# Attention output product of eleven instead of twelve passes through spare rows, and the filter's last feature products turned round, with their constants as weights

## The chip, the core and the metric

The kernel runs on one core of a Trainium2 chip. The metric is device time in microseconds (us) of one execution. Engines in the profile: PE (TensorE matmul) and PEld (its weight loads), DVE (VectorE), ACT (ScalarE), POOL (GpSimd) and SP (SyncE); POOL and SP here mainly issue DMAs.

## The reference

Two independent results are written side by side. The left half is attention of 16 heads with one shared key and value head; the right half is a spectral filter (a 2-D FFT, a product with a complex filter, the inverse FFT).

```python
B, S, D, H = 1, 2048, 448, 16           # head size Dh = 28
q = (x @ wq).reshape(B, S, H, Dh).transpose(0, 2, 1, 3)
k, v = x @ wk, x @ wv
p = softmax(einsum("bhqd,bkd->bhqk", q, k) * Dh ** -0.5)
a = einsum("bhqk,bkd->bhqd", p, v).transpose(0, 2, 1, 3).reshape(B, S, H * Dh) @ wo
...
X = rfft2(x2, axes=(-2, -1)) * (w_r + 1j * w_i)
b = irfft2(X, s=(S, D), axes=(-2, -1))
out = concatenate([a, b], axis=-1)
```

## The kernel before

**Layout.** The 16 heads are four groups g of four heads, each head padded from 28 to 32 rows, so that a group fills 128 partitions. The 2048 queries are four chunks c of 512. For each (c, g) the 2048 keys are 16 blocks kc of 128: 256 *steps* in all. A step has four score products (one a head, 128 keys by 512 queries, float32r, in `score`, L1100), four exponentials of 128 by 512 on ACT (`exps`, L1117, into a buffer `p`), and four value products (`values`, L1132, fp32, 32 rows each, into PSUM bank 7). Banks 0 to 6 are shared by scores and by filling work. There are `P_BUFS` = 20 buffers `p`; an exponential can't begin before its buffer and its scores are there, and a buffer is free again when the value products of its step have read it.

**Precision by parts.** Where a float32r product alone is too coarse, an operand is split into a high part and a remainder (`oh`, `ol` for the attention result, `woh`, `wol` for the output weights), and three products are added: high by high, remainder by high, high by remainder.

**Filling work.** Two kinds of work are put on PE between the scores. A *W unit* (`w_unit`, `wo_mm`, L1020) is the output product of 128 queries: four groups g, three float32r products of 448 columns each, twelve in all; DVE copies the bank out (L1024) and SP stores it. *Z and Y units* are the filter's last stage, for eight blocks q. Z (`z_unit`, L942): four fp32 products, weights are the filter data, moving are the constants `fi`; DVE copies the result to SBUF (L948). Y (`y_unit`, L961): the results of Z are the weights, the constants `cs3` (113 by 113) are moving, four fp32 products of 113 columns; DVE makes sums and differences (L966 to L968, L974, L975), and SP stores 128 rows of 4 by 113. Their buffers are carved out of `X`, the 28.9 KB a partition in which the filter's middle part ran on DVE until then.

**Order.** All engines run in a fixed order that the kernel's own planner writes while it is built: `clk` holds planned clocks, `after` a heap of planned events for DVE and DMA, `background` the filter's DVE work. The main loop at the end of the kernel issues scores while a bank is free, and value products in a batch of 2 steps, or of 4 when filling work is there (`size`). I call what lies between the starts of two batches a *round*: a short round has 8 scores and ends with the value products of 2 steps, a long one has 15 to 17 scores, filling work in two or three places, and ends with the value products of 4 steps. How much is filled in a long round is set by `share`: at least 1.6 us of planned time, more when the steps run out. At the end the third chunk's leftovers and 36 products of the last chunk (`partial`) follow the last value products.

**Around a group's end.** `group_out` (L986) copies bank 7 out, the sums of the exponentials go through DRAM (POOL's DMAs `sd`, `rs`, `rd`, `R`), and `group_norm` (L1008, L1010, L1011) multiplies and splits. When the fourth group of a chunk is done, the chunk's four W units can start.

Of the kernel before, what the change touches and what calls it, by code (L numbers as in the profile page):

```python
# [12 lines left out]
F32 = mybir.dt.float32  # L13
# [4 lines left out]
ALU = mybir.AluOpType  # L18
# [13 lines left out]
P_BUFS = 20  # L32
# [63 lines left out]
def kernel(ctx: ExitStack, tc: tile.TileContext, t: dict):  # L96
# [14 lines left out]
    X = cp.tile([128, 2, 32, 113], F32, name="X")  # L111
# [101 lines left out]
    with tc.tile_pool(name="f1", bufs=2) as f1[0], tc.tile_pool(name="w1", bufs=1) as w1, ExitStack() as ctx1:  # L213
# [146 lines left out]
        def load_const(name, shape):  # L360
            def go():
                cons[name] = cp.tile(shape, F32, name=name)
                nc.sync.dma_start(cons[name], t[name])
            return add(SP, 0.4, go, loads[1, 1], kb=32)
# [297 lines left out]
    pp = ctx.enter_context(tc.tile_pool(name="pp", bufs=P_BUFS))  # L662
    V = nc.vector
# [8 lines left out]
    def after(when, dur, f, *a):  # L672
        heapq.heappush(events, (when, next(serial), dur, f, a))
# [17 lines left out]
    woh = ap.tile([128, NG, D], F32R, name="woh", bufs=1)  # L691
    wol = ap.tile([128, NG, D], F32R, name="wol", bufs=1)
    fc["cs3"] = ap.tile([113, 4, 113], F32, name="cs3", bufs=1)
    nc.gpsimd.dma_start(fc["cs3"], t["cs3"])
# [66 lines left out]
    def wo_split(g):  # L761
        V.tensor_copy(woh[:, g], wo[g])
        TT(wol[:, g], wo[g], woh[:, g].bitcast(F32), op=ALU.subtract)
# [145 lines left out]
    Xf = X.rearrange("p r n f -> p (r n f)")  # L909
    taken = [0]  # L910

    def carve(p, n):
        o = taken[0]
        taken[0] += n
        return Xf[:p, o:o + n]

    c2t = [carve(128, 904).rearrange("p (u j f) -> p u j f", u=2, f=113) for _ in range(2)]
    fit = [carve(128, 512).rearrange("p (j f) -> p j f", f=128) for _ in range(2)]
    zt = [[carve(113, 512).rearrange("p (r j n) -> p r j n", r=2, n=64) for _ in range(2)] for _ in range(2)]
    mt = [carve(128, 226).rearrange("p (k f) -> p k f", f=113) for _ in range(2)]  # L920
    y1t = [carve(128, 452).rearrange("p (k h f) -> p k h f", k=2, f=113) for _ in range(2)]
    yot = [carve(128, 452).rearrange("p (k f) -> p k f", f=113) for _ in range(2)]
# [6 lines left out]
    def fft3_load(q):  # L929
        if q > 7:  # L930
            return
        nc.gpsimd.dma_start(c2t[q % 2].rearrange("p u j f -> p u (j f)"), t2[:, :, 452 * q:452 * q + 452])
        nc.gpsimd.dma_start(fit[q % 2], t["fi"][:, 4 * q:4 * q + 4])
        after(clk["dve"] + (10.0 if q < 2 else 6.0), 0.0, work["z"].extend, [z_unit(q, 0), z_unit(q, 1)])

    def z_unit(q, e):
        w = (113, 112)[e]

        def go(b):
            pz = view(bank[b], 4, 128)  # L940
            for j in range(4):
                mm(pz[:w, j], c2t[q % 2][:, e, j, :w], fit[q % 2][:, j], start=True, stop=True)  # L942
            if e == 1:
                after(clk["pe"] + 1.2, 0.0, fft3_load, q + 2)
            after(clk["pe"] + 1.2, 0.72, out, b)
# [6 lines left out]
        return [(0.88, go)]  # L952

    def y_unit(q, v):
        js = slice(2 * v, 2 * v + 2)

        def go(b):
            py = view(bank[b], 4, 113)
            ze, zo = zt[q % 2]
            for k, (z, w, r) in enumerate(((ze, 113, 0), (zo, 112, 0), (zo, 112, 1), (ze, 113, 1))):  # L960
                mm(py[:, k], z[:w, r, js], fc["cs3"][:w, k], start=True, stop=True)  # L961
            after(clk["pe"] + 1.2, 1.2, out, b)

        def out(b):
            py, m, y1 = view(bank[b], 4, 113), mt[v], y1t[v]
            V.tensor_copy(m, py[:, 2:4])  # L966
            TT(y1[:, :, 0], py[:, 0:2], m, op=ALU.add)
            TT(y1[:, :, 1], py[:, 0:2], m, op=ALU.subtract)  # L968
            free[b] = clk["dve"] + 0.1
            after(clk["dve"], 0.8, last)  # L970

        def last():
            y1, yo = y1t[v], yot[v]
            TT(yo[:, 0:2], y1[:, 0], y1[:, 1], op=ALU.add)  # L974
            TT(yo[:, 2:4], y1[:, 0], y1[:, 1], op=ALU.subtract)  # L975
            r0 = (2 * q + v) * 128
            nc.sync.dma_start(t["ob"][r0:r0 + 128], yo)
        return [(0.88, go)]


    oh, ol, osb = {}, {}, {}
# [13 lines left out]
    def group_sums(c, g, rs, rd):  # L995
        V.reciprocal(rs, rs)
        nc.gpsimd.dma_start(rd.rearrange("i (a b) -> (i a) b", b=16), rs)
        R = ap.tile([128, CW], F32, name="R", bufs=1)
        for i in range(4):
            nc.gpsimd.dma_start(R[32 * i:32 * i + 32], rd[i:i + 1].to_broadcast([32, CW]))  # L1000
        after(clk["dve"] + 12.0, 2.1, group_norm, c, g, R)

    def group_norm(c, g, R):
# [4 lines left out]
        TT(o, o, R, op=ALU.mult)  # L1008
        h = oh[c][:, g]
        V.tensor_copy(h, o)  # L1010
        TT(ol[c][:, g], o, h.bitcast(F32), op=ALU.subtract)  # L1011
        normed[c] += 1
        if normed[c] == NG and c < NC - 1:
            after(clk["dve"] + 0.3, 0.0, work["w"].extend, [w_unit(c, k) for k in range(4)])

    def wo_mm(p, c, k, gs):
        s = slice(k * 128, k * 128 + 128)
        for g in gs:
            for n, (x, w) in enumerate(((oh, woh), (ol, woh), (oh, wol))):
                mm(p, x[c][:, g, s], w[:, g], start=(g == 0 and n == 0), stop=(g == NG - 1 and n == 2))  # L1020
# [20 lines left out]
    def w_unit(c, k):  # L1041
# [10 lines left out]
        return [(0.605, go(g)) for g in range(NG)]  # L1052
# [102 lines left out]
    for g in range(NG):  # L1155
        after(w0 + 6 * g, 0.0, wo_load, g)
        after(w0 + 6.0 + 6 * g, 1.1, wo_split, g)
# [81 lines left out]
    nc.sync.dma_start(w3, t["wo"][:, g])  # L1239
# [25 lines left out]
def _constants():  # L1265
# [27 lines left out]
    c["cs3"] = np.stack([we * np.cos(te.T), pad(2.0 / D * np.cos(to.T)), pad(-2.0 / D * np.sin(to.T)),  # L1293
                         -we * np.sin(te.T)], 1)
# [14 lines left out]
def _layout(A_x, A_wq, A_wk, A_wv, A_wo, B_x, B_w_r, B_w_i):  # L1309
# [13 lines left out]
    z["wo"] = wo.reshape(NG, 128, D).transpose(1, 0, 2)  # L1323
# [18 lines left out]
def _gather(oa, ob):  # L1342
    out = np.empty((1, S, 2 * D), np.float32)
    out[0, :, :D] = oa
    y = ob.reshape(32, 64, 4, 113).transpose(1, 0, 2, 3).reshape(S, 4, 113)
# [9 lines left out]
_OUTS = {"oa": (S, D), "ob": (S, 4, 113)}  # L1355
# [16 lines left out]
```

## Time and profile before

| | us |
|---|---|
| runs (three) | 641.3, 644.09, 645.07 |
| median | 644.09 |
| profiled execution, device time | 641.98 |
| its span | 640.1 |
| first value products start | 76.31 |
| last value products start | 624.04 |

The granted clock of PE was 0.999 over the span. In rows of the timeline the columns are start, duration, engine, line, operation, output and inputs, shapes, count, and in brackets how long the engine stood idle before it and what ended that. A PE matmul's duration includes its way through the array; what a stream of them costs is read from start to start.

### The profile page before, as it was taken

How to read it: one execution, taken by the hardware profiler on the slowest of the kernel's cores; microseconds unless marked ns; L12 is line 12 of the kernel's file. 1: busy time of each engine (PE TensorE's matmuls, PEld its weight loads, DVE VectorE, ACT ScalarE, POOL GpSimd, SP SyncE). 2: the span in 40 equal slices, each digit the busy share in tenths (PEclk: the TensorE clock that was granted, in tenths of full speed). 3: DMA queues.
4: the chain of work that ended last, by engine and by line, in shares of the span. 5: the costliest groups of instructions: out<-in, count | busy, mean ns of one | idle time of the engine just before them, and what ended most of it. 6: DMA issues, size and time to landing. Idle time of an engine off the chain costs nothing.

```text
span 640.1 us, 11636 instructions
## 1 busy us (share of the span) xinstructions
PE 633.5 (99%) x4380; PEld 358.5 (56%) x4380; DVE 333.3 (52%) x687; ACT 547.0 (85%) x1100; POOL 89.1 (14%) x164
## 2 busy tenths in 40 slices
PE   9999999999999999999999999999999999999997
PEld 7877544444444456554446655655665655564445
DVE  5999615979897977896323222215334310320014
ACT  4644899999999998889999879878888987888991
POOL 1021131101121101010122020020301101020200
PEclk9999999999999999999999999999999999999999
DMA  8766587030334121124444231132415131130002
GB/s 299 255 164 166 134 239 244 18 68 17 97 105 102 42 68 47 32 67 150 151 141 139 64 91 36 49 111 88 115 61 143 32 82 32 50 93 1 19 0 87
DMA packets 29667, 62.41 MB, mean 98 GB/s; under 512 B 6798, under 2 KB 18415, under 8 KB 28645
## 3 DMA queue, kind: packets, MB, share of 16 engines
q1 hardware_dynamic: 21850, 40.36, 23.1%
q0 software_dynamic: 7328, 20.72, 10.8%
q8 instruction: 35, 0.57, 0.4%
q10 hardware_dynamic: 432, 0.57, 0.3%
q14 instruction: 22, 0.18, 0.1%
HBM read 29.63 MB, written 15.02 MB: 70 GB/s over the span
## 4 chain that ended last, share of the span: by engine, by line
PE 88%; ACT 0%; issue 0%; DVE 0%; ACTq 0%
PE b L1100 41%; PE b L1132 36%; PE b L1020 6%; PE b L961 2%; PE b L942 2%; PE b L1252 0%; PE b L163 0%; ACT yb L1035 0%; DVE yb L1038 0%; ACTq L1036 0%
## 5 line engine op out<-in xcount | busy, mean ns | idle before, releaser
L1117 ACT ACTIVATE p<-b 128x512 f32<-128x512 f32 x1024 | 506.7, 768 | 46.4 <-PE b L1100 45.4
L1100 PE MATMUL b<-qa,ka 128*128 128x512 f32 x1024 | 284.7, 411 | 0.5 <-PEq L617 0.5
L1100 PEld LDWEIGHTS b<-qa,ka 128*128 128x128 f32 x1024 | 182.1, 188 | 128.2 <-ACT p L1117 83.9
L1132 PE MATMUL b<-p,vs 128*32 128x512 f32 x2048 | 240.0, 597 | 0.0
L1132 PEld LDWEIGHTS b<-p,vs 128*32 128x32 f32 x2048 | 56.5, 109 | 120.9 <-issue 119.3
L986 DVE COPY qraw<-b 128x512 f32<-128x512 f32 x15 | 10.4, 692 | 82.0 <-PE b L1132 82.0
L1024 DVE COPY ya<-b 128x448 f32<-128x448 f32 x12 | 7.5, 624 | 65.1 <-PE b L1020 64.0
L991 POOL DMA_DIRECT2D sd<-qraw x15 | 8.8, 587 | 218.8 <-DVE qraw L986 218.8
L827 DVE SCALAR_TENSOR_TENSOR X<-w,X 128x226 f32<-128x226 f32 (+2 forms) x72 | 34.1, 473 | 2.4
L1000 POOL DMA_DIRECT2D R<-rd x60 | 30.2, 508 | 34.9 <-DMA rd<-rs 34.9
L966 DVE COPY X<-b 128x226 f32<-128x226 f32 x16 | 6.2, 390 | 45.3 <-ACT p L1117 43.9
L321 ACT ACTIVATE qraw<-b 128x512 f32<-128x512 f32 x16 | 9.4, 599 | 19.5 <-PE b L317 19.4
L948 DVE COPY X<-b 113x512 f32<-113x512 f32 (+1 forms) x16 | 11.1, 691 | 28.6 <-ACT p L1117 22.7
L317 PE MATMUL b<-xh,wqh 128*128 128x512 f32 x64 | 24.6, 416 | 0.4 <-DVE xh L265 0.4
L1008 DVE TENSOR_TENSOR qraw<-qraw,R 128x512 f32<-128x512 f32 x15 | 10.3, 685 | 26.7 <-DMA R<-rd 26.7
L317 PE MATMUL b<-xh,wql 128*128 128x512 f32 x64 | 23.0, 390 | 0.0
L1020 PE MATMUL b<-woh,oh 128*128 128x448 f32 x60 | 22.1, 369 | 0.0
L1020 PE MATMUL b<-wol,oh 128*128 128x448 f32 x60 | 22.0, 366 | 0.0
L1020 PE MATMUL b<-woh,ol 128*128 128x448 f32 x60 | 21.9, 366 | 0.0
L820 DVE SCALAR_TENSOR_TENSOR w<-X 128x113 f32<-128x113 f32 (+2 forms) x56 | 17.7, 353 | 0.1
L961 PEld LDWEIGHTS b<-cs,X 113*128 113x128 f32 (+1 forms) x128 | 16.8, 191 | 1.4
L317 PE MATMUL b<-xl,wqh 128*128 128x512 f32 x48 | 17.3, 391 | 0.0
(113 smaller groups left out, 511.4 us busy)
## 6 DMA issues: line engine op xcount, KB each, us to landing
qa<-qa SPq DMA_DIRECT2D x15, 512.0 KB
X<-t POOLq DMA_DIRECT2D x16, 452.0 KB, 5.4
xb<-xb SPq DMA_DIRECT2D x8, 512.0 KB
qa<-qh SPq DMA_DIRECT2D x60, 64.0 KB
qa<-ql SPq DMA_DIRECT2D x60, 64.0 KB
R<-rd POOLq DMA_DIRECT2D x60, 64.0 KB, 2.2
t<-bs SPq DMA_DIRECT2D x16, 226.0 KB
wf<-w POOLq DMA_DIRECT2D x8, 452.0 KB, 4.2
```

The source lines that it names most:

```text
L317: mm(pq[c, g], w[:, j, gs], x[:, j], start=(j == 0 and n == 0), stop=(j == 3 and n == 1))
L820: STT(out, y, sy, x, op0=ALU.mult, op1=ALU.add if c > 0 else ALU.subtract)
L827: todo(226 * n, lambda d=d, q=q: STT(both(d), t[0].rearrange("p r n f -> p r (n f)"), q, both(a), op0=ALU.mult, op1=ALU.add))
L942: mm(pz[:w, j], c2t[q % 2][:, e, j, :w], fit[q % 2][:, j], start=True, stop=True)
L948: V.tensor_copy(zt[q % 2][e][:w], view(bank[b], 4, 128)[:w].rearrange("p j (r n) -> p r j n", r=2))
L961: mm(py[:, k], z[:w, r, js], fc["cs3"][:w, k], start=True, stop=True)
L986: V.tensor_copy(o, bank[7])
L1000: nc.gpsimd.dma_start(R[32 * i:32 * i + 32], rd[i:i + 1].to_broadcast([32, CW]))
L1020: mm(p, x[c][:, g, s], w[:, g], start=(g == 0 and n == 0), stop=(g == NG - 1 and n == 2))
L1100: mm(bank[b], ka[:, kc * 128:(kc + 1) * 128], qa[c, g][:, h], start=True, stop=True)
L1117: nc.scalar.activation(p, bank[b], AF.Exp, scale=SCALE)
L1132: mm(bank[7][32 * i:32 * i + 32], vs[:, kc], pt.pop(4 * st + i), start=(kc == 0), stop=(kc == 15))
```

## The change

**Output product.** In chunks 0 to 2 the third product of group 0 (remainder `ol` of group 0 by `woh` of group 0) is dropped. Its 112 real rows are carried by the 4 unused rows in each block of 32 of seven other operands: the remainder of group 0 goes to DRAM (`lows`) and comes back by eight DMAs on SP into rows 28 to 31 of `oh` (all four groups) and of `ol` (groups 1 to 3), and the weights hold the matching rows of group 0, which needs seven weight blocks in `woh` in place of four. A W unit has eleven products. It may start 7 planned us after the last group of its chunk is normalised. Chunk 3 keeps twelve.

**Filter.** In Y the constants, now split into `csh` and `csl` and padded to 128 columns, are the weights; the results of Z, split by DVE into a high part and a remainder, are moving. A Y unit is six float32r products of 256 columns. Both Y units of a block are needed for the last sums, which now are 128 by 512; two stores of 128 rows of 2 KB follow per block. The constants come by a POOL DMA when the filter's middle part has ended, and are split on DVE.

**Memory and planner.** `X` has its space only until the last stage begins, `P_BUFS` is 17, some constants move to an early pool, and the planner's numbers for W, Y and Z are new, with at least 1.8 us in a long round in place of 1.6.

```diff
-P_BUFS = 20
+P_BUFS = 17
...
-    woh = ap.tile([128, NG, D], F32R, name="woh", bufs=1)
+    woh = ap.tile([128, 7, D], F32R, name="woh", bufs=1)
...
+    def fft3_open():
+        xp.close()
+        p3 = xp.enter_context(tc.tile_pool(name="p3", bufs=2))
...
+        cs = scratch()[:, :512].rearrange("p (k f) -> p k f", k=4)
+        nc.gpsimd.dma_start(cs, t["cs3"])
+        todo(512, lambda: V.tensor_copy(csh, cs))
+        todo(512, lambda: TT(csl, cs, csh.bitcast(F32), op=ALU.subtract))
...
-            V.tensor_copy(zt[q % 2][e][:w], view(bank[b], 4, 128)[:w].rearrange("p j (r n) -> p r j n", r=2))
+            pz = view(bank[b], 4, 128)[:w].rearrange("p j (r n) -> p r j n", r=2)
+            h, l = (x[:w] for x in fb["z", q % 2, e])
+            V.tensor_copy(h, pz)
+            TT(l, pz, h.bitcast(F32), op=ALU.subtract)
...
-            for k, (z, w, r) in enumerate(((ze, 113, 0), (zo, 112, 0), (zo, 112, 1), (ze, 113, 1))):
-                mm(py[:, k], z[:w, r, js], fc["cs3"][:w, k], start=True, stop=True)
+            for k in range(2):
+                kind, e, r = ((0, 0, 0), (2, 1, 1), (1, 1, 0), (3, 0, 1))[2 * v + k]
...
+                for n, (c, z) in enumerate(((csh, zh), (csh, zl), (csl, zh))):
+                    mm(py[:, k], c[:w, kind], z, start=(n == 0), stop=(n == 2))
...
+            if g == 0:
+                lows[c] = dp.tile([128, CW], F32, name="lows", bufs=2)
+                nc.sync.dma_start(lows[c], ol[c][:, 0].bitcast(F32))
+            rows = lows[c].rearrange("(i m r) n -> r i m n", i=4, r=4)
+            if g == NG - 1:
+                for r in range(4):
+                    nc.sync.dma_start(oh[c][DH + r::32].bitcast(F32), rows[r, :, :4])
+                    nc.sync.dma_start(ol[c][DH + r::32, 1:].bitcast(F32), rows[r, :, 4:7])
+                after(clk["dve"] + 7.0, 0.0, work["w"].extend, [w_unit(c, k) for k in range(4)])
...
-            for n, (x, w) in enumerate(((oh, woh), (ol, woh), (oh, wol))):
-                mm(p, x[c][:, g, s], w[:, g], start=(g == 0 and n == 0), stop=(g == NG - 1 and n == 2))
+            spare = c < NC - 1
+            for n, (x, w, m) in enumerate(((oh, woh, g), (oh, wol, g), (ol, woh, g + 3 * spare))):
+                if n < 2 or g or not spare:
+                    mm(p, x[c][:, g, s], w[:, m], start=(g == 0 and n == 0), stop=(g == NG - 1 and n == 2))
...
-    total = 12 * 4 * 0.605 + 32 * 0.88
+    total = 12 * 2.22 + 16 * (0.88 + 0.73)
...
-        return max(1.6, n * (total - done[0]) / max(250 - done_steps, 3)) if n > 2 else 0.0
+        return max(1.8, n * (total - done[0]) / max(250 - done_steps, 3)) if n > 2 else 0.0
```

**What it does to the order.** ACT's order is the same throughout; PE's is the same up to step 80. From there the planner packs differently. PE's order, first long round before (`qa`, `ka` are the operands of a score, `b` the banks; the row ahead of the first three output products is the sixth score after the value products):

```order
L1100 MATMUL b_77<-qa_1163,ka 128x512
L1020 MATMUL b_80<-woh,oh 128x448
L1020 MATMUL b_80<-woh,ol 128x448
L1020 MATMUL b_80<-wol,oh 128x448
L1100 MATMUL b_78<-qa_1163,ka 128x512
L1100 MATMUL b_79<-qa_1163,ka 128x512
L1020 MATMUL b_80<-woh,oh 128x448
```

The same place now, from the sixth score of the first long round:

```order
L1124 MATMUL b_77<-qa_1167,ka 128x512
L1044 MATMUL b_78<-woh,oh 128x448
L1044 MATMUL b_78<-wol,oh 128x448
L1124 MATMUL b_80<-qa_1167,ka 128x512
L1124 MATMUL b_81<-qa_1167,ka 128x512
L1044 MATMUL b_78<-woh,oh 128x448
L1044 MATMUL b_78<-wol,oh 128x448
L1044 MATMUL b_78<-woh,ol 128x448
L1124 MATMUL b_82<-qa_1167,ka 128x512
```

The first group's third product is gone, and a round now holds a whole W unit in four places (2, 3, 3 and 3 products) where it held three places of three.

PE's order at the first Y units, before (`X` is where the results of Z lie):

```order
L1100 MATMUL b_78<-qa_128,ka 128x512
L961 MATMUL b_80<-cs_1092,X 128x113 x4
L1100 MATMUL b_82<-qa_128,ka 128x512
L1100 MATMUL b_83<-qa_128,ka 128x512
L961 MATMUL b_81<-cs_1092,X 128x113 x4
```

and now (`zh`, `zl` are the parts of the results of Z):

```order
L1124 MATMUL b_82<-qa_127,ka 128x512
L972 MATMUL b_77<-zh_3809,csh 128x256
L972 MATMUL b_77<-zl_3810,csh 128x256
L972 MATMUL b_77<-zh_3809,csl 128x256
L972 MATMUL b_77<-zh_3811,csh 128x256
L972 MATMUL b_77<-zl_3812,csh 128x256
L972 MATMUL b_77<-zh_3811,csl 128x256
L1124 MATMUL b_78<-qa_127,ka 128x512
L1124 MATMUL b_76<-qa_127,ka 128x512
L972 MATMUL b_81<-zh_3811,csh 128x256
```

Four products became six of another shape; behind the second unit, which begins in the last row, a Z unit follows as a third place in the same round.

DVE's order where the filter's middle part ends, now (`qraw<-qraw,R` begins `group_norm`, `qt<-qraw` begins the split of the next group's queries, `qraw<-b_83` is `group_out`):

```order
L829 SCALAR_TENSOR_TENSOR X<-w,X 128x2x113 x2
L923 CAST csh<-w 128x512
L924 TENSOR_TENSOR csl<-w,csh 128x512
L1022 TENSOR_TENSOR qraw<-qraw,R 128x512
L1024 CAST oh<-qraw 128x512
L1025 TENSOR_TENSOR ol<-qraw,oh 128x512
L195 TENSOR_SCALAR qt<-qraw,mask,cvec 128x512
L196 CAST qh<-qt 128x512
L197 TENSOR_TENSOR ql<-qt,qh 128x512
L1001 COPY qraw<-b_83 128x512
```

The two rows of `csh` and `csl` stand ahead of a group's norm and of the next `group_out`; before, they were not there.

Counted over the whole order of PE, with S scores, W output products, and Y and Z units in a long round:

| | before | now |
|---|---|---|
| short rounds | 68 | 82 |
| long rounds | 30 | 23 |
| stretches of long rounds, by first steps | 80, 128, 208 | 84, 128, 134, 144, 212 |
| output products in long rounds | 141 (47 places) | 129 (12 places of 2, 35 of 3) |
| output products after the last score | 6 + 33 | 3 + 36 |

The long rounds now: 6 of S16 W11 (three of them open a stretch), 2 of S17 W11, 2 of S16 YYZ (one opens a stretch), S15 YYZ, S17 YYZ, S16 ZZZ (opens a stretch), S17 ZZZ, 2 of S15 Z W5, 2 of S16 W6 Y, 2 of S16 Y W8, S16 W3 ZZ, S16 YYY, S15 Y ZZ. Before: 6 of S15 W9, 6 of S15 YY, 2 of S16 W9, 6 of S16 with W6 and a Y or Z, 3 of S17 W9, 5 of S17 ZZ, 2 of S17 W3 ZZ.

More of the change, by code (lines that the diff above doesn't have):

```diff
@@ L952, in z_unit @@
         return [(0.88, go)]
+    y1 = {}
     def y_unit(q, v):
-        js = slice(2 * v, 2 * v + 2)
         def go(b):
-            py = view(bank[b], 4, 113)
-            ze, zo = zt[q % 2]
-            for k, (z, w, r) in enumerate(((ze, 113, 0), (zo, 112, 0), (zo, 112, 1), (ze, 113, 1))):
-                mm(py[:, k], z[:w, r, js], fc["cs3"][:w, k], start=True, stop=True)
-            after(clk["pe"] + 1.2, 1.2, out, b)
-        def out(b):
[L965 to L970, printed above, removed]
@@ new lines, in go @@
+            after(clk["pe"] + 1.2, 2.65 if v else 1.25, out, b)
+        def out(b):
+            py = view(bank[b], 2, 256)
+            y = y1[v] = scratch()[:, :768].rearrange("p (s n) -> p s n", s=3)
+            V.tensor_copy(y[:, 2], py[:, 1])
+            TT(y[:, 0], py[:, 0], y[:, 2], op=ALU.add)
+            TT(y[:, 1], py[:, 0], y[:, 2], op=ALU.subtract)
+            free[b] = clk["dve"] + (-1.3 if v else 0.1)
+            if v:
+                a, c = y1.pop(0), y1.pop(1)
+                for h, op in enumerate((ALU.add, ALU.subtract)):
+                    last(h, op, a, c)
@@ L982, with last @@
+        def last(h, op, a, c):
+            yo = fp.tile([128, 2, 256], F32, name="yo", tag="bs")
+            TT(yo, a[:, :2], c[:, :2], op=op)
+            nc.sync.dma_start(t["ob"][q, h], yo)
+        return [(0.73, go)]
+    oh, ol, osb, lows = {}, {}, {}, {}
+    R = ap.tile([128, CW], F32, name="R", bufs=1)
+    after(12.0, 0.4, V.memset, R, 0.0)
     normed, taken_out = [0] * NC, [0]
@@ L1012, in group_norm @@
         normed[c] += 1
-        if normed[c] == NG and c < NC - 1:
-            after(clk["dve"] + 0.3, 0.0, work["w"].extend, [w_unit(c, k) for k in range(4)])
+        if c < NC - 1:
+            if g == 0:
[7 more added lines that the diff above has]
+                after(clk["dve"] + 7.0, 0.0, work["w"].extend, [w_unit(c, k) for k in range(4)])
     def wo_mm(p, c, k, gs):
@@ L1051, in out @@
             free[b] = clk["dve"] + 0.1
-        return [(0.605, go(g)) for g in range(NG)]
+        return [(0.605 if g else 0.403, go(g)) for g in range(NG)]
     def switch(mode):
@@ L1154 @@
     w0 = 5.0 if FIRST == 8 else 28.0
-    for g in range(NG):
-        after(w0 + 6 * g, 0.0, wo_load, g)
-        after(w0 + 6.0 + 6 * g, 1.1, wo_split, g)
+    for g in range(7):
+        at = w0 + 6 * g if g < NG else 60.0 + 6 * g
+        after(at, 0.0, wo_load, g)
+        after(at + 6.0, 1.1, wo_split, g)
     for q in range(FIRST, 8):
```

73 lines of the change are left out of this document (34 added, 39 removed).

## The prediction

> **What bounds the kernel now.** The page first: PE's share, and the chain that ended last.
>
> ```profile
> span 640.1 us, 11636 instructions
> PE 633.5 (99%) x4380; PEld 358.5 (56%) x4380; DVE 333.3 (52%) x687; ACT 547.0 (85%) x1100; POOL 89.1 (14%) x164
> PE 88%; ACT 0%; issue 0%; DVE 0%; ACTq 0%
> ```
>
> Read alone, this says that PE is the bound and that each us of PE work taken away is a us won. The timeline says otherwise for a part of the run. A short round on PE, and in the second fence ACT over that part:
>
> ```profile
> 123.46 1.92 PE L1132 MATMUL b<-p,vs 128*32 128x512 f32 x16
> 125.31 2.11 PE L1100 MATMUL b<-qa,ka 128*128 128x512 f32 x8
> 127.36 1.92 PE L1132 MATMUL b<-p,vs 128*32 128x512 f32 x16
> ```
>
> ```profile
> 75.69 163.84 ACT L1117 ACTIVATE p<-b 128x512 f32<-128x512 f32 x334
> ```
>
> From 75.69 on ACT runs 334 exponentials without a gap, 0.49 us each; a short round is eight of them, 127.36 - 123.46 = 3.90 (3.96 later on; I take 3.93). There **ACT** is the bound. A long round of 15 scores:
>
> ```profile
> 359.46 3.64 PE L1132 MATMUL b<-p,vs 128*32 128x512 f32 x32
> 363.03 1.67 PE L1100 MATMUL b<-qa,ka 128*128 128x512 f32 x6
> 363.57 5.99 ACT L1117 ACTIVATE p<-b 128x512 f32<-128x512 f32 x12 [1.16 <-PE b L1100]
> 364.54 0.37 PE L1020 MATMUL b<-woh,oh 128*128 128x448 f32 x1
> 364.75 0.36 PE L1020 MATMUL b<-woh,ol 128*128 128x448 f32 x1
> 365.62 0.36 PE L1020 MATMUL b<-woh,oh 128*128 128x448 f32 x1
> 368.14 0.19 PEld L1100 LDWEIGHTS b<-qa,ka 128*128 128x128 f32 x1 [0.20 <-ACT p L1117]
> 368.57 0.64 PE L1132 MATMUL b<-p,vs 128*32 128x512 f32 x4
> ```
>
> It lasts 9.11. Value products hold PE for 3.57 (359.46 to 363.03), ACT runs dry and starts again 4.11 after the round's start. But the last score also waits 0.20 for a bank, which an exponential frees. So a long round has two bounds: PE's own sum, and a **tick of ACT**: 4.11, plus one exponential (5.99 for twelve, 0.50) for each score beyond the banks that scores can use (six while a filling unit holds one), plus the rest to 9.11, 0.50, from the bank to the value products. With 15, 16, 17 scores that is 9.11, 9.61, 10.11. Two more rounds, of 16 and (second fence) of 17 scores:
>
> ```profile
> 246.66 3.64 PE L1132 MATMUL b<-p,vs 128*32 128x512 f32 x32
> 255.34 0.19 PEld L1100 LDWEIGHTS b<-qa,ka 128*128 128x128 f32 x1 [0.19 <-ACT p L1117]
> 255.83 0.19 PEld L1100 LDWEIGHTS b<-qa,ka 128*128 128x128 f32 x1 [0.30 <-ACT p L1117]
> 256.27 1.06 PE L1132 MATMUL b<-p,vs 128*32 128x512 f32 x8
> ```
>
> ```profile
> 416.06 3.64 PE L1132 MATMUL b<-p,vs 128*32 128x512 f32 x32
> 426.16 3.64 PE L1132 MATMUL b<-p,vs 128*32 128x512 f32 x32
> ```
>
> 9.61 and 10.10, as the tick has it. Without its waits, 0.19 and 0.30, PE would have needed 9.12 in the first, a little more since a load's wait is partly covered by the product before it; I take 9.15. So some 0.4 of it is not PE's work at all. PE's gain therefore counts only where PE's sum is over the tick.
>
> **The excess of long rounds.** I price all by what long rounds cost beyond short ones for the same steps. Their three stretches, from short batch to short batch:
>
> ```profile
> 229.24 1.92 PE L1132 MATMUL b<-p,vs 128*32 128x512 f32 x16
> 280.89 1.92 PE L1132 MATMUL b<-p,vs 128*32 128x512 f32 x16
> 332.37 1.93 PE L1132 MATMUL b<-p,vs 128*32 128x512 f32 x16
> 515.96 1.92 PE L1132 MATMUL b<-p,vs 128*32 128x512 f32 x16
> 519.86 1.92 PE L1132 MATMUL b<-p,vs 128*32 128x512 f32 x16
> 580.75 1.92 PE L1132 MATMUL b<-p,vs 128*32 128x512 f32 x16
> ```
>
> They last 51.65, 183.59 and 60.89 for 22, 78 and 26 steps, that is 11, 39 and 13 short rounds at 3.93: excess 8.4 + 30.3 + 9.8 = 48.5, 1.6 for each of 30 long rounds.
>
> **The prices of the pieces.** A W place costs what it adds: 365.62 - 364.54 = 1.08 with two scores, and a score is 0.22 (2.11 for eight, 1.67 for six, above), so 0.64, of which three products take 0.205 each (364.54 to 364.75, rounded); a place of two is 0.435. PE's sum of 16 scores without filling is 9.15 less three places, 7.23. Y units:
>
> ```profile
> 431.23 1.04 PE L961 MATMUL b<-cs,X 113*128 113x113 f32 x8
> 432.04 0.71 PE L1100 MATMUL b<-qa,ka 128*128 128x512 f32 x2
> 432.59 1.04 PE L961 MATMUL b<-cs,X 113*128 113x113 f32 x8
> ```
>
> 1.36 with two scores, so 0.92; Z, also eight fp32 records a unit, is taken the same. A float32r product of 256 columns is not in this trace. From below it is 256/448 of 0.205, 0.117, with no fixed part; from above the 0.205 of 448 columns. I take 0.125, near the lower end, since the eight weight loads of a Y unit, as wide as the new ones, come every 0.101 (431.23 to 432.04) and so don't hold it up. Y is then 6 x 0.125 + 0.03 = 0.78, the 0.03 being what a W place has beyond its products.
>
> The Trainium skill ("TensorE: Matmul & The Clock Gate", Back-to-back issue gap) has a warm product cost N/2.4 + 2.5 ns, 189 ns for 448 columns. The trace has 205, so I keep the trace; by the page Y would be 0.09 cheaper and the sum about 1.5 us lower.
>
> PE's filling work in long rounds goes from 47 x 0.64 + 32 x 0.92 = 59.5 to 12 x 0.435 + 35 x 0.64 + 16 x 0.78 + 16 x 0.92 = 54.8: **4.7 less**, 2.5 by W (12 products), 2.2 by Y.
>
> **The new rounds.** Now the larger of PE's sum and tick. S16 W11: PE 7.23 + 0.435 + 1.92 = 9.59, tick 9.61. YYZ 9.71 (S15 9.49, S17 tick 10.11). Z W5 with S15: tick 9.11. W6 Y: tick 9.61. Y W8 9.73. W3 ZZ 9.71. S17 ZZZ 10.21. S17 W11: tick 10.11. YYY 9.61, YZZ with S15 9.63. The 18 rounds inside stretches sum to 174.4, 9.7 each. The five that open a stretch have ACT busy throughout:
>
> ```profile
> 237.06 1.50 PE L1132 MATMUL b<-p,vs 128*32 128x512 f32 x12
> ```
>
> ```profile
> 275.22 3.64 PE L1132 MATMUL b<-p,vs 128*32 128x512 f32 x32
> ```
>
> 237.06 - 229.24 = 7.82 with 15 scores, 8.3 with 16. The first short round behind a stretch was 5.67 (275.22 to 280.89) with six scores ahead; now seven are ahead, which takes away up to one exponential; I take half of it, 5.42. Together 174.4 + 41.5 + 27.1 = 243.0 for 102 steps, 51 short rounds (200.4): **excess 42.6 in place of 48.5**. That is 5.9 won; with 3.96 for the twelve short rounds that come instead, 5.5; I take 5.4, since no round can be better than its tick. It is more than PE's work because 23 rounds, not 30, pay the tick. One more W place falls behind the last value products, +0.6.
>
> **Costed at nothing, with their cover.** DVE gets 16 remainders of Z (0.69 each, as the first row of the second fence; 11 us), three casts, one fill and two splits. Its share where the filling is thick (columns: stretch, length, then busy PE, PEld, DVE, ACT, POOL), and the place where the constants come in:
>
> ```profile
> 400.00:450.00 50.00, 50.00 (x333) 30.25 (x326) 14.60 (x29) 41.05 (x84) 6.70 (x12) 1.00 0.29 83
> ```
>
> ```profile
> 322.85 0.69 DVE L1008 TENSOR_TENSOR qraw<-qraw,R 128x512 f32<-128x512 f32 x1 [12.86 <-DMA R<-rd]
> 334.36 0.69 DVE L986 COPY qraw<-b 128x512 f32<-128x512 f32 x1 [7.99 <-PE b L1132]
> ```
>
> DVE is busy 14.6 of 50 there, so only a late copy could hurt: a bank held one tick longer is 0.5. `csh` waits for a DMA behind the filter's last store on POOL's queue, and a norm, the next queries and `group_out` stand behind it on DVE. Before, DVE stood still 12.86 at that place anyway, and then had 7.99 to spare before `group_out`. So up to 8 us of a later landing are free, all beyond that is PE's. The eight DMAs from `lows` on SP wait for `ol` and block only the next group's queries, due a group later; the first W place follows the norm (end 223.25) by 9 us before and a short round more now:
>
> ```profile
> 222.56 0.69 DVE L1011 TENSOR_TENSOR ol<-qraw,oh 128x512 fp32r<-128x512 f32 x1
> 232.58 0.37 PE L1020 MATMUL b<-woh,oh 128*128 128x448 f32 x1
> ```
>
> **Buffers, 17 for 20.** Short rounds use 8 + 7 = 15. In a long round 16 are held by the batch, so one exponential, not four, can run ahead:
>
> ```profile
> 427.30 1.57 ACT L1117 ACTIVATE p<-b 128x512 f32<-128x512 f32 x3 [0.17 <-PE b L1132]
> 430.26 5.99 ACT L1117 ACTIVATE p<-b 128x512 f32<-128x512 f32 x12 [1.39 <-PE b L1100]
> ```
>
> A buffer comes free 1.14 after the batch starts (426.16 to 427.30). The other six then end at 1.14 + 6 x 0.50 = 4.14, and new scores reach ACT at 4.11. The idle 1.39 covers it, to a few hundredths; from nothing to 0.86 a round (a step of value products later) is possible. I take nothing.
>
> **Sum.** 640.1 - 5.4 + 0.6 = span 635.3; with the 1.9 around the span, 637.2 against this execution's 641.98. That execution lies 2.1 under the median of the three runs, from which the same sum gives 639.3. I predict 638.2, between.
>
> **Rivals.** *Buffers bind* (slower): the cover above is gone if a buffer comes back later than 1.14, and wholly if ACT has to wait for the next step: 0.86 in each of 16 long rounds with seven scores ahead is 13.8, so 652. Against it: the 1.14 is measured. 9 in 100. *Narrow float32r is dear* (slower): if 256 columns cost what fp32 does in the Y rows, 0.2025 for 113 columns, a unit is 2.8 and 16 of them add 32, 670; at 0.205 a product it is 1.26, 0.48 over my price, +7.7, 646. From 0.15 a product the gain in Y is lost. 6 in 100 in all, half for each. *Ticks eat it* (no change): places late in a round leave two banks held, and the long rounds get 0.3 longer in the mean: 23 x 0.3 = 7, 645. For it: the tick decided most rounds before. 14 in 100. *DVE late* (no change): constants or copies late by 5 beyond their cover, 643. 8 in 100, and 1 more for over 8 late, slower. *More is won*: a W unit ends in its round, its bank comes back before the last score, the tick drops by one and openings are 7.9: 634. 12 in 100. *Forecast*: 5 in 10.
>
> A rule that speaks for still more: the Trainium skill (same page, The mechanism) lets a weight load overlap running products only in other row groups. Then a Y unit would go from eight loads and streams to six. This trace denies it: loads of 0.19 sit inside spacings of 0.101 and 0.205. It gets no chance of its own beyond the last rival's.
>
> **Numbers.** Half a per cent, 3.2, is about what a measurement can tell: faster means under 640.9. Forecast and more-is-won give faster 0.59 (a fifteenth of the forecast's 0.50 goes to no change); no change 0.14 + 0.08 + 0.03 + 0.03 = 0.28; slower 0.09 + 0.03 + 0.01 = 0.13. The range goes from the better rival to ticks and narrow products at 646: 633.5 to 646.
>
> **What would show it.** Y's six products at 0.12 to 0.13 each. Long rounds of W11 at 9.6, none over 10.2. ACT idle for about 1.1 behind each long batch's start, none when the new scores come. `csh` waiting for its DMA and `group_out` not late. Last value products near 618.7, 16.7 before the end. The forecast is wrong if long rounds of 16 scores last 10 or more, or if a round waits for DVE or a DMA.

## The result and the profile after

The changed kernel takes 637.95 us in the median of seven runs (635.8 to 640.77), the kernel before 644.75 (seven runs beside them, 641.3 to 646.03). The ratio is **0.9904, 95% interval 0.9881 to 0.9927**: faster by 1%. The profiled execution took 635.8, its span is 633.1. Of the page after, the span, the busy time of the engines, and the shares of the chain that ended last, by engine:

```profile
span 633.1 us, 11646 instructions
...
PE 626.6 (99%) x4336; PEld 351.5 (56%) x4336; DVE 347.3 (55%) x693; ACT 546.5 (86%) x1100; POOL 90.5 (14%) x167
...
PE 88%; ACT 0%; issue 0%; DVE 0%; ACTq 0%
```

The page reads as it did before: PE is busy for 99% of the span, and the chain is PE's alone. It doesn't show what changed; the rounds do. The timeline of PE after, a round of 16 scores with a whole W unit of eleven, from value products to value products (columns: start, duration, engine, line, operation, shapes, count):

```profile
254.16 3.64 PE L1156 MATMUL b<-p,vs 128*32 128x512 f32 x32
257.73 1.66 PE L1124 MATMUL b<-qa,ka 128*128 128x512 f32 x6
259.23 0.36 PE L1044 MATMUL b<-woh,oh 128*128 128x448 f32 x1
259.43 0.36 PE L1044 MATMUL b<-wol,oh 128*128 128x448 f32 x1
259.63 0.61 PE L1124 MATMUL b<-qa,ka 128*128 128x512 f32 x2
...
262.83 1.09 PE L1124 MATMUL b<-qa,ka 128*128 128x512 f32 x4
263.85 0.64 PE L1156 MATMUL b<-p,vs 128*32 128x512 f32 x4
```

It lasts 9.69, and behind its first scores no load in it waits as long as 0.1 for ACT: PE's sum decides, by a hair. The Y units, and behind the second one a Z unit, in the round from step 134 on:

```profile
357.18 0.28 PE L972 MATMUL b<-zh,csh 113*128 113x256 f32 x1
357.30 0.28 PE L972 MATMUL b<-zl,csh 113*128 113x256 f32 x1
...
357.78 0.28 PE L972 MATMUL b<-zh,csl 112*128 112x256 f32 x1
357.90 0.63 PE L1124 MATMUL b<-qa,ka 128*128 128x512 f32 x2
358.37 0.29 PE L972 MATMUL b<-zh,csh 112*128 112x256 f32 x1
```

Six products in 0.72, 0.12 each; with two scores 1.19 (357.18 to 358.37) where the old unit had 1.36. Less 0.44 for the scores that is 0.75. ACT after, the start of three long batches:

```profile
245.67 7.97 ACT L1141 ACTIVATE p<-b 128x512 f32<-128x512 f32 x16 [1.62 <-PE b L1156]
255.31 7.97 ACT L1141 ACTIVATE p<-b 128x512 f32<-128x512 f32 x16 [1.66 <-PE b L1156]
265.00 7.97 ACT L1141 ACTIVATE p<-b 128x512 f32<-128x512 f32 x16 [1.72 <-PE b L1156]
```

ACT now stands still once in most long rounds, until a buffer comes back from the value products (1.15 behind the batch's start, 254.16 to 255.31), and then does 16 exponentials without a gap. Before, it also stood still about once in a long round, but until new scores came; only in six places did it stop for a buffer, for 0.2 at most. Its waits summed (the page of waits; columns: what waited, for whom, us in total, times, longest), after and, in the second fence, before:

```profile
ACT p L1141 <- PE b L1156: 28.7, 18, 2.0
...
ACT p L1141 <- issue: 8.5, 5, 1.8
...
ACT p L1141 <- PE b L1124: 3.7, 7, 1.1
```

```profile
ACT p L1117 <- PE b L1100: 45.4, 31, 1.7
...
ACT p L1117 <- PE b L1132: 1.0, 6, 0.2
```

DVE at the end of the filter's middle part, and in the second fence the first and the last value products:

```profile
322.06 0.43 DVE L923 CAST csh<-w 128x512 fp32r<-128x512 f32 x1 [10.04 <-DMA w<-cs]
...
331.99 0.69 DVE L1001 COPY qraw<-b 128x512 f32<-128x512 f32 x1 [5.34 <-PE b L1156]
```

```profile
75.45 1.07 PE L1156 MATMUL b<-p,vs 128*32 128x512 f32 x8
...
616.83 0.64 PE L1156 MATMUL b<-p,vs 128*32 128x512 f32 x4
```

The constants were waited for, `group_out` still waited for PE and not the other way round. From the first to the last value products (I call this **the loop**) it is 616.83 - 75.45 = 541.38, before 624.04 - 76.31 = 547.73. The loop is 6.35 shorter, the tail behind it 0.2 longer, and 0.86 of the difference of the two spans lies ahead of the loop.

### The profile page after: what moved, and what is told of

It is laid out like the page before. It is cut to its first block, busy times and chain, and to the rows that moved or that the text cites. A ratio compares the mean times of both kernels' runs of the same rounds, so it can differ in the third digit from the quotient of the medians.

```text
span 633.1 us, 11646 instructions
## 1 busy us (share of the span) xinstructions
PE 626.6 (99%) x4336; PEld 351.5 (56%) x4336; DVE 347.3 (55%) x693; ACT 546.5 (86%) x1100; POOL 90.5 (14%) x167
## 4 chain that ended last, share of the span: by engine, by line
PE 88%; ACT 0%; issue 0%; DVE 0%; ACTq 0%
PE b L1124 41%; PE b L1156 37%; PE b L1044 5%; PE b L946 2%; PE b L972 2%; PE b L1277 0%; PE b L162 0%; ACT yb L1059 0%; DVE yb L1062 0%; ACTq L1060 0%
## 5 line engine op out<-in xcount | busy, mean ns | idle before, releaser
L978 DVE COPY w<-b 128x256 f32<-128x256 f32 x16 | 6.8, 424 | 36.6 <-PE b L972 35.0
L316 PE MATMUL b<-xh,wqh 128*128 128x512 f32 x64 | 23.7, 401 | 0.4 <-DVE xh L264 0.4
L316 PE MATMUL b<-xh,wql 128*128 128x512 f32 x64 | 23.0, 389 | 0.0
L954 DVE CAST zh<-b 113x512 fp32r<-113x512 f32 (+1 forms) x16 | 11.0, 689 | 16.5 <-ACT p L1141 11.0
L1044 PE MATMUL b<-woh,ol 128*128 128x448 f32 x48 | 17.5, 364 | 0.0
L316 PE MATMUL b<-xl,wqh 128*128 128x512 f32 x48 | 17.3, 390 | 0.0
L865 DVE TENSOR_TENSOR w<-X,wf 128x904 f32<-128x904 f32 x16 | 17.0, 1097 | 0.3
```

The lines of the kernel that those rows point to most:

```text
L316: mm(pq[c, g], w[:, j, gs], x[:, j], start=(j == 0 and n == 0), stop=(j == 3 and n == 1))
L865: TT(u[r], both(s), wt[k][:, r:r + 1].to_broadcast([128, 2, 452]), op=ALU.mult)
L954: V.tensor_copy(h, pz)
L1044: mm(p, x[c][:, g, s], w[:, m], start=(g == 0 and n == 0), stop=(g == NG - 1 and n == 2))
```

## The experiments

The loop is the instrument. What lies ahead of it differs from one execution to the next: the first value products came between 75.45 and 80.46. The latest, that of experiment 6, by stretches (columns: stretch, length, then busy PE, PEld, DVE, ACT, POOL, granted clock of PE, share of DMA, GB/s):

```profile
60.00:75.00 15.00, 13.98 (x239) 10.19 (x231) 12.92 (x30) 9.38 (x18) 2.37 (x5) 0.88 0.47 114
75.00:100.00 25.00, 25.00 (x149) 12.41 (x147) 8.55 (x17) 23.34 (x49) 7.57 (x14) 0.94 0.86 238
```

From 60 to 75 the granted clock was 0.88 there, in the profile of the changed kernel it was 1.00. That is only a part of the 5.0: in experiment 2 the clock of that stretch was 0.89, and the first value products came at 76.88; and in experiment 6 PE was 2.3 behind before the clock fell (the same `b<-xh,wqh` of L316 started at 61.57 there and at 59.24 in the changed kernel, and the clock was 1.00 up to 70). What made it late by then stays open. The loop repeats much better: two kernels with PE's order of before gave 547.73 and 547.71, two with the order after 541.38 and 541.47. All runs, with the ratio to the kernel before (three rounds each):

| run | ratio, 95% interval | loop | expected by the theory |
|---|---|---|---|
| before | 1 | 547.73 | |
| after | 0.9904, 0.9881 to 0.9927 | 541.38 | 542.4 |
| 1 twelve, same order | 0.9928, 0.9897 to 0.996 | 543.41 | 542.6 |
| 2 eight in Y | 0.9931, 0.9902 to 0.996 | 544.70 | 544.3 to 544.6 |
| 3 four places alone | 0.9971, 0.9946 to 0.9996 | 546.04 | 545.2 to 546.7 |
| 4 before, 17 buffers | 1.0013, 0.9986 to 1.004 | 547.71 | 547.7 |
| 5 sixteen buffers | 0.9913, 0.9884 to 0.9941 | 542.32 | 540 to 543 |
| 6 constants by SP | 0.9905, 0.9872 to 0.9938 | 541.47 | 541.4 |
| 7 one place in short rounds | 1.0011, 0.9985 to 1.0037 | 548.09 | 528 to 539 |
| 8 output product alone | 0.9939, 0.9918 to 0.996 | 544.16 | 543.7 |
| 9 filter alone | 0.9946, 0.9921 to 0.997 | 544.12 | 544.3 |
| 10 turned in fp32 | 0.9913, 0.9879 to 0.9947 | 543.35 | 543 to 544 |

**1. The twelfth product back, in the same order.**

```diff
-            spare = c < NC - 1
+            spare = False
```

> The changed kernel in its own order on PE, but with the product of group 0 put back, so that a W unit has twelve products again (the spare rows are carried as well, so the output is too large by that part). Theory (a long round is the larger of PE's sum and ACT's tick): 0.205 is added to each of the twelve W units, and shows only in rounds that PE's sum decides: 3 of S16 W11 inside stretches and 2 of Y W8 get 0.2 each, 2 of S15 Z W5 0.1 each, the S17 W11 rounds and the openings nothing. From first to last value products 541.4 becomes 542.6. Rival (PE is the bound everywhere): 12 x 0.205 = 2.5, 543.9. Rival (nothing but the number of long rounds counts): 541.4.

The loop grew by 2.03. The W round at step 92, which with eleven products lasts 9.69:

```profile
259.36 3.64 PE L1156 MATMUL b<-p,vs 128*32 128x512 f32 x32
269.25 1.06 PE L1156 MATMUL b<-p,vs 128*32 128x512 f32 x8
```

The three W11 rounds inside the first stretch went from 9.63, 9.69 and 9.70 to 9.91, 9.89 and 9.89, the two of Y W8 from 9.80 to 9.98, as the theory has it; the S17 W11 rounds by 0.05 and 0.07, the opening at step 84 by 0.01. But the openings at 144 and 212 grew by 0.29 and 0.21 (7.90 to 8.19, 8.00 to 8.21), and the two of Z W5 by 0.2. So the theory was right in kind and held too few rounds to be PE's: 2.03 lies between its count of 1.2 and the rival's 2.5, and nearer the rival's, since nine of the twelve products show nearly in full. Of the openings of the change, the one at 212 has no load behind its first scores that waits longer than 0.12 for ACT, while at 84 two do, 0.24 and 0.30:

```profile
240.18 0.19 PEld L1124 LDWEIGHTS b<-qa,ka 128*128 128x128 f32 x1 [0.24 <-ACT p L1141]
...
244.10 0.19 PEld L1124 LDWEIGHTS b<-qa,ka 128*128 128x128 f32 x1 [0.30 <-ACT p L1141]
```

**2. Two more products in Y.**

```diff
-for n, (c, z) in enumerate(((csh, zh), (csh, zl), (csl, zh))):
+for n, (c, z) in enumerate(((csh, zh), (csh, zl), (csl, zh), (csl, zl))):
...
```

> The changed kernel with a fourth product for each half of a Y unit (low part by low part), eight of 256 columns in place of six, same order. Theory: 0.12 a product, 0.24 a unit, so that Y costs 1.03, and it shows in rounds that PE's sum decides: 12 of 16 units there (YYZ 2 x 0.24 in three rounds, YYY 0.72, YZZ 0.24, two YW8 0.24 each), nothing in the two W6Y rounds, at most 0.3 in the opening YYZ: from first to last value products 541.4 becomes 544.3 to 544.6. Rival (PE is the bound everywhere): 3.9, 545.3. Rival (tick decides): within 0.5 of 541.4.

3.32 more, a little over the forecast: the opening with YYZ grew by 0.49 (8.07 to 8.56) where at most 0.3 was expected. The round of YYY went from 9.65 to 10.34, YYZ at 138 from 9.82 to 10.28, the two W6Y rounds from 9.60 to 9.61 and 9.68. The round of YYY:

```profile
447.03 3.64 PE L1156 MATMUL b<-p,vs 128*32 128x512 f32 x32
457.37 1.06 PE L1156 MATMUL b<-p,vs 128*32 128x512 f32 x8
```

The new product costs 0.12 and is paid where the round is PE's; a Y at its old price of 0.92, 0.17 over 0.75, would so cost some 3.3 x 0.17 / 0.24 = 2.3 in this order (an estimate).

**3. Four places, no cheaper work.**

```diff
-        return max(1.6, n * (total - done[0]) / max(250 - done_steps, 3)) if n > 2 else 0.0
+        return max(1.9, n * (total - done[0]) / max(250 - done_steps, 3)) if n > 2 else 0.0
```

> The kernel before with only the planner's least share raised from 1.6 to 1.9: four W places (twelve products) or three Y and Z units in a long round, 24 long rounds in place of 30, 80 short ones in place of 68; no work is taken off PE. Theory: without the cheaper units PE's sum takes over (W12 9.79, YYZ 9.99), the 19 rounds inside stretches sum to 186.7, five openings 41, five firsts behind 28.3, an excess of 47.7 in place of 48.5; with short rounds of 3.91 where no unit is left open 1 to 1.5 more: 1 to 2.5 faster than before. Rival (the gain is that of fewer long rounds): 5 to 6 faster, as the change. Rival (packing alone costs): slower by 2.

1.69 shorter than before, inside the forecast: the smaller number of long rounds (24 for 30) is not the gain by itself. Its W12 rounds last 9.91 to 9.92, and 10.13 to 10.21 those of 16 scores with three Y and Z units, where the theory had 9.79 and 9.99: PE's sum without filling is 7.35 (9.91 less four places of 0.64) and not 7.23. With no W unit left open, its short rounds take 3.90 to 3.91, also where they took 3.96 before.

**4. The kernel before with 17 buffers.**

```diff
-P_BUFS = 20
+P_BUFS = 17
```

> The kernel before with 17 buffers p in place of 20, same order on PE. Theory: the buffers are covered, at most 0.03 a long round: same within 1. Rival (the wait for a buffer delays the exponentials of a long round): 0.1 to 0.86 in each of 30 long rounds, 3 to 13 slower.

547.71 for 547.73, and no round moved by more than 0.07. In the order of before the buffers are covered.

**5. Sixteen buffers.**

```diff
-P_BUFS = 17
+P_BUFS = 16
```

> The changed kernel with 16 buffers p in place of 17; the planner then puts one score of an opening behind the value products. Theory: in a batch all 16 are held, ACT starts 1.14 after a batch begins and needs 16 exponentials (8.0) and the 0.50 from bank to value products, 9.64 a round whatever it holds, which is what PE's sum takes in most rounds anyway: the two S15 Z W5 rounds rise from 9.11 to 9.6, the S17 ones fall: same within 1.5. Rival (each buffer taken away costs ACT one exponential a long round): 0.5 x 23 = 11 slower than the changed kernel.

0.94 more, of which 0.82 is a last round that holds two W places in place of one (3.72 for 2.90). The W11 rounds stay at 9.68 to 9.70, Z W5 rises from 9.13 to 9.59 and S17 W11 falls from 10.08 to 9.69, as forecast. But these rounds now hold 16 scores each, since the planner put one score of an opening behind the value products, and for 16 scores the tick of the prediction, 9.61, says nearly the same; so the run doesn't separate ACT's sum from the number of scores. ACT again does 16 exponentials a round after the wait for a buffer:

```profile
256.85 8.03 ACT L1141 ACTIVATE p<-b 128x512 f32<-128x512 f32 x16 [1.71 <-PE b L1156]
```

So one buffer less cost some 0.1 here beside the last round; what ACT must do in a round, 1.65 + 8.0, is as long as PE's sum.

**6. The constants by another queue.**

```diff
-        nc.gpsimd.dma_start(cs, t["cs3"])
+        nc.sync.dma_start(cs, t["cs3"])
```

> The changed kernel with the constants' DMA on SP's queue in place of POOL's, where it stood behind the filter's last store and the broadcasts of a norm. Theory: csh lands earlier, DVE's wait of 10.0 there becomes shorter, and nothing changes in the time since group_out still waits for PE: same within 0.5. Rival (the late constants push the norm, the queries and group_out): up to 2 faster.

The same loop. Counted from the first value products `csh` began 4.6 earlier (322.44 - 80.46 against 322.06 - 75.45), and DVE stood idle longer ahead of `group_out`:

```profile
322.44 0.43 DVE L923 CAST csh<-w 128x512 fp32r<-128x512 f32 x1 [5.39 <-DMA w<-cs]
...
337.02 0.69 DVE L1001 COPY qraw<-b 128x512 f32<-128x512 f32 x1 [9.60 <-PE b L1156]
```

**7. No long rounds: a place in each short round.** A miss.

```diff
-        b = 4 if rich else 2
+        b = 2
...
-        return max(1.8, n * (total - done[0]) / max(250 - done_steps, 3)) if n > 2 else 0.0
+        return max(1.8, n * (total - done[0]) / max(250 - done_steps, 3)) if n > 2 else 0.3
```

> The changed kernel with batches of 2 steps throughout: one filling place in each short round from step 82 to 252, and no long round. Theory (a round is the larger of PE's sum and ACT's tick; the tick of a short round, 3.8 with six banks, is under ACT's 3.91): PE's sum of an empty short round is half of 7.23, up to 0.13 more for the second change from value products to scores, so W3 4.26 to 4.40, W2 4.05 to 4.19, Y 4.40 to 4.53, Z 4.54 to 4.67: excess 32 to 43 in place of 45: 2 to 13 faster than the changed kernel, 625 to 636. Rival (long batches are needed, since a bank held by filling starves ACT in each short round by 0.5): 80 x 0.5 = 40 in place of what PE adds, or both together, 640 or more.

6.7 more than the change. A short round with W3 lasts 4.50 where 4.26 to 4.40 was expected. PE and, in the second fence, ACT of this run:

```profile
260.87 1.92 PE L1156 MATMUL b<-p,vs 128*32 128x512 f32 x16
262.72 1.66 PE L1124 MATMUL b<-qa,ka 128*128 128x512 f32 x6
...
264.82 0.62 PE L1124 MATMUL b<-qa,ka 128*128 128x512 f32 x2
265.37 1.92 PE L1156 MATMUL b<-p,vs 128*32 128x512 f32 x16
```

```profile
258.76 4.03 ACT L1141 ACTIVATE p<-b 128x512 f32<-128x512 f32 x8 [0.28 <-PE b L1124]
263.26 4.03 ACT L1141 ACTIVATE p<-b 128x512 f32<-128x512 f32 x8 [0.47 <-PE b L1124]
```

The time lies where the rival had it, 640 or more, but not for its reason: ACT waits 0.47 for scores, PE has no gap in the round, so PE is late and ACT is not starved by a bank. 4.52, the mean of its 36 W3 rounds, less a W place of 0.64 is 3.88 for an empty short round of PE, and two of them are 7.75, against 7.35 for a long one with the same scores and steps. By this estimate each further change from scores to value products and back costs 0.4 of PE, three times the 0.13 that I had allowed. Of it 0.13 lies in the value products (2 x 1.85 against 3.57), the rest among the scores.

**8 and 9. Each part alone.** Number 8 is the kernel before with the hunks of the diff on `P_BUFS`, `woh`, `lows`, `R` and `wo_mm` and a share of 1.8; number 9 is the changed kernel with

```diff
-            spare = c < NC - 1
+            spare = False
...
-        return [(0.605 if g else 0.403, go(g)) for g in range(NG)]
+        return [(0.605, go(g)) for g in range(NG)]
...
-    total = 12 * 2.22 + 16 * (0.88 + 0.73)
+    total = 12 * 2.42 + 16 * (0.88 + 0.73)
...
-        return max(1.8, n * (total - done[0]) / max(250 - done_steps, 3)) if n > 2 else 0.0
+        return max(1.9, n * (total - done[0]) / max(250 - done_steps, 3)) if n > 2 else 0.0
```

and without `lows` and its DMAs, so that W units start as before.

> The kernel before with the output product's part of the change alone (eleven products by spare rows, 17 buffers) and the planner's share of 1.8; the filter's last stage as before. Theory, with the rounds measured so far (W11 9.7, YYZ with the old Y 10.15, Z or Y with two W places 9.6): 18 rounds inside stretches 175.8, six openings 48.9, six firsts behind 34.3, an excess of 48.0 over short rounds of 3.91, where four places alone had 50.3: from first to last value products 543.7, that is 4.0 less than before and 2.3 less than four places alone. Rival (ticks hide the products saved): as four places alone, 546.0. Rival (the DMAs into the spare rows come late): over 546.

> The changed kernel with twelve output products and no spare rows, and a share of 1.9, so that four W places still go into a long round: the filter's part of the change alone. Theory, with the rounds measured so far (W12 9.92, YYZ 9.81, YYY 9.65, Y or Z with two W places 9.6): 18 rounds inside stretches 176.4, six openings 49.1, six firsts behind 34.1, an excess of 48.6: from first to last value products 544.3, 3.4 less than before and 1.7 less than four places alone. Rival (the filter's part brings nothing beyond the order): 546.0. Rival (it is most of the change): 542 or less.

544.16 and 544.12. Over the order alone (3) each part brings 1.9, both together 4.7. The parts alone still need 24 long rounds in six stretches, where the whole change has 23 in five; that the 0.9 more is this round and stretch is an argument, not a run.

**10. Turned round, but in fp32.**

```diff
-for n, (c, z) in enumerate(((csh, zh), (csh, zl), (csl, zh))):
-    mm(py[:, k], c[:w, kind], z, start=(n == 0), stop=(n == 2))
+mm(py[:, k], csh[:w, kind].bitcast(F32), zh.bitcast(F32), start=True, stop=True)
```

> The changed kernel with each half of a Y unit as one fp32 product of 256 columns on the high parts alone (remainders of the constants and of Z's results left out), in place of three float32r ones; same order. It prices the turning round without the splitting. Theory (an fp32 product of 128 columns took 0.23 in the Z rows, so 0.43 to 0.46 for 256): a Y unit costs 0.86 to 0.95 in place of 0.75, and 13 of 16 units show it: from first to last value products 541.4 becomes 543 to 544. Rival (the load, not the columns, sets the price of fp32 in Y): under 0.3 a product, 541.4 or less.

1.97 more than the change. The unit with its two scores, in this run:

```profile
359.59 1.03 PE L971 MATMUL b<-zh,csh 113*128 113x256 f32 x4
360.27 0.82 PE L1123 MATMUL b<-qa,ka 128*128 128x512 f32 x2
360.92 1.03 PE L971 MATMUL b<-zh,csh 112*128 112x256 f32 x4
```

1.33, against 1.36 with the constants moving and 1.19 in three float32r products. Turning the product round gains almost nothing by itself, 0.03 a unit; the gain comes with the three float32r products. That these need the wider moving operand, 256 columns for 113, to beat one of fp32 is an argument: no run has float32r the old way round.

None of these versions beats the change. By the prices measured a long round of 16 scores is filled best with 9.61 - 7.35 = 2.26; 54.8 of filling then take 24.2 such rounds, each 1.79 over two short ones of 3.91, 43.4 in all. The change stands at 45 by the same count (244.3 less 51 short rounds of 3.91), so by this estimate packing has little left to give.

## Why the prediction was right, and where its terms were off

**The mechanism holds.** A long round is the larger of PE's sum and ACT's tick: experiments 1, 2 and 10 put work into rounds without moving anything else, and the time came where PE's sum decides and stayed away where the tick does. The fall of the excess was forecast as 5.9, of which 5.4 were taken, and came as 4.6 (48.5 before; 244.3, the first three rows below, less 51 short rounds of 3.93); the loop as a whole fell by 6.35, 1.0 more than forecast. The terms were off both ways: the first three rows cost 1.3 more than forecast, the short rounds and the last round gave 1.4 and 0.8 more.

That the median, 637.95, comes within 0.3 of the 638.2 is luck. The forecast was 4.8 less than a base of 643.0, which I had set between one execution and the median of three. The base of the seven runs is 644.75, 1.75 higher, and the gain was 6.8 by the medians; loop and tail together give 6.15, and the rest of the difference of the two spans lies ahead of the loop.

| term | predicted | measured |
|---|---|---|
| 18 rounds inside stretches | 174.4 | 175.4 |
| five openings | 41.5 | 40.7 |
| five first short rounds behind | 27.1 | 28.2 |
| short rounds elsewhere | 3.93, twelve at 3.96 | 3.91, ten at 3.96 |
| last round | as before, 3.74 | 2.90 |

**PE's sum of 7.23** was too small by 0.12. I had taken 9.15 for a round of 9.61 with waits of 0.19 and 0.30, since a load's wait "is partly covered by the product before it"; more of it was covered than I took. By the rounds that PE decides it is 7.35 (experiment 3). That makes the W11 rounds 9.69 for 9.61 and most of the 1.0 in the first row.

**The first short round** was taken as 5.42, from the one score more that now lies ahead. All five are 5.62 to 5.68, the first one before was 5.67. They are PE's. One of the change, and in the second fence one of before that holds nine scores and is followed by the value products at 515.96:

```profile
273.55 3.64 PE L1156 MATMUL b<-p,vs 128*32 128x512 f32 x32
277.12 2.14 PE L1124 MATMUL b<-qa,ka 128*128 128x512 f32 x8
279.19 1.92 PE L1156 MATMUL b<-p,vs 128*32 128x512 f32 x16
```

```profile
510.09 3.64 PE L1132 MATMUL b<-p,vs 128*32 128x512 f32 x32
513.66 2.37 PE L1100 MATMUL b<-qa,ka 128*128 128x512 f32 x9
```

Value products of four steps take 3.57, eight scores with their change 2.07, nine 2.30: one score more in the round adds what a score costs PE. One more ahead shortened nothing. This step failed, and it cost 1.1.

**The tick of 17 scores**, 10.11, I had read off one round. Of the other eight long rounds of 17 scores before, seven lasted 9.59 to 9.61 and one 9.84 (435.26 to 444.85 is one of the seven). The rule has them so if a seventh bank is free for scores, but the prediction didn't say which rounds those are. For the two S17 W11 it came right: 10.09 and 10.08.

**The short rounds elsewhere** brought 0.9 against 3.93 throughout, where I had set 0.5 aside for rounds of 3.96. Without an open unit a short round takes 3.91, with a bank held by one 3.96; 13 short rounds behind the first stretch lost their open unit. In the change only those from step 234 to 252 have one:

```profile
574.36 1.92 PE L1156 MATMUL b<-p,vs 128*32 128x512 f32 x16
578.31 1.92 PE L1156 MATMUL b<-p,vs 128*32 128x512 f32 x16
```

3.95 here; where none is open, the mean of eleven is 3.91 (steps 190 to 210). In experiments 3, 8 and 9, which leave none open, it is 3.90 to 3.91 up to the end.

**The last round** was not in the sum at all. It is PE's and holds one score and one W place fewer than before, 0.22 + 0.64 = 0.86, and became 0.84 shorter. The W place moved from there to behind the last value products, and the sum had only that half, +0.6. Even that came smaller: 33 products took 6.91 there and 36 take 7.31, 0.4 more, and the tail as a whole grew by 0.2.

**Y at 0.78** with 0.125 a product is 0.75 with 0.12. The rule of the Trainium skill ("TensorE: Matmul & The Clock Gate", Back-to-back issue gap) gives 109 ns for 256 columns; the trace has 120, between that and my price, and the trace decides. Six products came one behind the other at that pace though each has a load of its own, of 0.19 over 113 or 112 rows, such as

```profile
357.31 0.19 PEld L972 LDWEIGHTS b<-zh,csl 113*128 113x128 f32 x1
```

The Trainium skill (same page, The mechanism) lists an overlap of loads with running products only where the row groups differ; here it is shown for the new products, which all use the same rows.

**Buffers, 17 for 20**, cost nothing, as I took it (experiment 4). I had shown that with the idle before new scores as cover, and feared "a few hundredths"; experiment 5 shows the cover to be wider, since PE's sum is as long as ACT's round with a wait for a buffer in it. Experiment 4 has the old order; no run has the new one with more than 17 buffers.

**The constants and DVE** cost nothing (experiment 6), and `group_out` kept 5.34 of the 7.99 that it had to spare.

**The rivals.** *Ticks eat it* fell: no round inside is 0.3 over forecast. *Narrow float32r* fell by the 0.12. *Buffers bind* and *DVE late* fell by experiments 4 and 6. *More is won* was half right on the openings (7.9 and 8.0 in the two with W11 behind 142 and 210, PE's sum) and wrong on the tick. What was not weighed at all is how much the long batch itself is worth to PE, 0.4 a round; experiment 7 failed on it. The prediction was not touched by that, since it compared long rounds with long ones.

## What to carry to other kernels

Where two engines alternate as the bound, price an edit round by round, as the larger of two sums, and count only the rounds in which the edited engine's sum is the larger; a page that says 99% busy can't tell them apart. Compare executions over a stretch that starts behind the noisy part: here a start that varied by 5 us hid differences of 1 us that the loop repeats to 0.1. A product that changes nothing else is a good probe of what a round is bound by: add one and see which rounds move.

## What the runs showed of the hardware that was not expected

- PE pays for each change between fp32 value products and float32r scores: some 0.4 for one more pair in the same work (7.75 against 7.35, an estimate from experiments 3 and 7), although PE counts as busy throughout.
- Three float32r products of 256 columns took 0.36, one of fp32 of the same shape some 0.07 more with what it holds up behind it (1.33 against 1.19 for two of them with two scores).
- A short round that is ACT's lasts 3.96 while an open unit holds one of the seven banks, and 3.91 where none does, eight exponentials in each. ACT's exponentials there stand without a gap in the trace: each is a little longer from start to start (0.495 against 0.489). Why is not shown.
- The granted clock of PE in the stretch from 60 to 75 was 1.00 in one execution and 0.88 in another. The first value products came 5 us later there, of which 2.3 were lost before the clock fell.
